# Order of VectorE, GpSimd and opening steps in a two-layer long-convolution and GEGLU kernel

## The chip, the cores and the metric

One core of a Trainium2 chip. The metric is the device time of one execution in microseconds; the runs give 977.12 as the median of three.

## The reference

Two layers run one after the other on `x` (1 x 2048 x 576, bf16). Each layer first gates the normalized `x` with a long convolution, then adds a GEGLU feed-forward. The convolution `y` depends on `A_k`, `A_v` and the filters alone, so both layers use the same `y`.

```python
def _A_ref(q, k, v, shift_k, ssm_k, ssm_D):        # long convolution, gated by q
    k_shift = sum over t of k_pad[:, t:t + S, :] * shift_k[:, ks - 1 - t]   # ks = 4 taps
    kv = k_shift * v
    y = irfft(rfft(kv, 2 * S) * rfft(ssm_k, 2 * S))[:, :S] + kv * ssm_D
    return q * y
def _B_ref(x, w_gate, w_up, w_down):               # 576 -> 4608 -> 576
    return (_gelu(x @ w_gate) * (x @ w_up)) @ w_down
for _ in range(2):
    x = x + _A_ref(_layernorm(x), A_k, A_v, A_shift_k, A_ssm_k, A_ssm_D)
    x = x + _B_ref(_layernorm(x), B_w_gate, B_w_up, B_w_down)
```

## The kernel before

**Units and visits.** The 2048 tokens are four blocks of 512. A unit is a layer and a block, in the order (0,0) (0,1) (1,0) (1,1) (0,2) (0,3) (1,2) (1,3), called unit 0 to unit 7 here. Five passes hold units 0; 1 and 2; 3 and 4; 5 and 6; 7. In each pass the 36 column tiles of the feed-forward are gone through in three parts of twelve; within a part, each unit of the pass is visited once, so there are 24 visits. A visit has twelve gate-and-up tiles ("gu", 18 matmuls each, line 1087), each followed by a GELU on ScalarE (line 1091, tile `ga`) and a product on VectorE (line 1092, tile `hT`), and then four groups of 24 down-projection matmuls ("dn", line 1103), one group for each 128 tokens.

**What a unit needs first.** Before its first visit, each of the four 128-token rows of a unit goes through: two VectorE gate steps with the convolution's `y` (lines 855 and 862, the second also sums the row), the mean's negative `nm` on GpSimd (line 819), a square with a sum on ScalarE (line 827, tile `junk`), `ve` and `rstd` on GpSimd (lines 834 and 835), a normalization `xn` and a short copy on VectorE (lines 888 and 890), and two DMA transposes from SP's queue into `xnT` (line 918). All four rows must have landed before the unit's first gu matmul. Layer 1 has the same steps, with a temporary `g_t`.

**The convolution.** It is a block FFT made of matmuls. For block m: the taps and the product with `v` on VectorE (lines 160 to 170, tiles `kvt` and `v`), forward transforms on TensorE (line 205), whose results ScalarE copies (line 208, `eo`) and VectorE combines (line 213, `kc`); products of spectra on VectorE (lines 222 to 226, `prod` and `sum`, spectra `kr` and `hr` loaded by GpSimd's DMAs, lines 316 and 324); accumulation on TensorE (line 232); and inverse transforms (line 258) copied to `y` (line 260). TensorE's share of this is put between matmuls of the feed-forward. Block 0 is done in the opening, block 1 during unit 0, blocks 2 and 3 later.

**The order.** A planner in Python, run while the program is built, writes the order out. It keeps a modelled time for TensorE, VectorE and ScalarE (`Pace`), with a constant cost for each step (`C_TINY` for a small GpSimd step). VectorE work waits in two lists: `conv.V` with the convolution's steps and `vq` with gates and normalizations. After each gu tile and each pair of dn matmuls `fill` takes from both, as long as modelled VectorE time allows; its argument `conv_first` says which list is asked first. Small GpSimd steps, spills of spectra and output stores wait in `conv.spills` with a due time and are put out by `flush` when modelled TensorE time has reached it. The weight loads (`load_wgu`, 12 tiles' worth in three buffers, lines 745 to 747; `load_wd`, line 755) stand in SP's queue along with the transposes.

```python
hurry = lambda: (1, RT - 1) not in conv.y_at            # block 1's y is not there yet
fill(t.pe + C_GU + LEAD, hurry(), hurry())              # after each gu tile
fill(t.pe + 1.5, True, hurry())                         # after each pair of dn matmuls
```

**The opening** (`Conv.begin`, lines 472 to 673) is ordered by hand: block 0's convolution, spectra of the filter for all four blocks (`h_tile`, matmuls of line 184, copied by ScalarE at line 186, stored to DRAM by GpSimd's queue at line 263; four buffers, so that a later `h_tile` waits for an earlier store), and unit 0's gates and normalizations. There `gate0(j)` does the two gate steps, the mean, the square and the root of row j; `norm0(j)` the normalization (lines 997 and 999); `turn0(j)` transposes it on TensorE (line 1009), with copies of the result (lines 1010 and 1012) on ScalarE or VectorE. One ScalarE table load for GELU is set off by the activation at line 653.

Of the kernel before, what the change touches and what calls it, by code (L numbers as in the profile page):

```python
# [18 lines left out]
P = 128  # L19
# [10 lines left out]
C_GU, C_DN = 1.944, 0.245  # L30
C_PR = 1.25
C_BF, C_TB = 0.37, 0.46
C_SQ, C_TINY = 0.85, 1.0
N_KC, N_SM = 4, 6
C_TT, C_ST, C_BN, C_NORM, C_HT, C_GELU, C_EVA, C_EVD = 0.76, 0.82, 0.47, 0.62, 0.69, 0.6, 0.66, 0.76
LAG = 0.25
HOLD, LEAD = 14.0, 1.8


# [15 lines left out]
class Conv:  # L55
# [9 lines left out]
    def __init__(self, tc, ctx, pace, A_k, A_v, A_shift_k, A_ssm_k, A_ssm_D, ident, psp, cpsp, ypool):  # L65
        self.tc, self.nc, self.t = tc, tc.nc, pace
        self.k2, self.v2, self.hk = A_k[0], A_v[0], A_ssm_k
        self.S, self.D = self.k2.shape
        self.NB = self.S // BS
        self.KS = A_shift_k.shape[1]  # L70
        self.sk, self.sD = A_shift_k, A_ssm_D
        self.ident, self.psp, self.cpsp, self.ypool = ident, psp, cpsp, ypool
        D = self.D
        pool = lambda name, bufs: ctx.enter_context(tc.tile_pool(name=name, bufs=bufs))
        self.cst = pool("c_cst", 1)
        self.krp = pool("c_kr", 3)
        self.hrp = pool("c_hr", 4)
        self.kcp = pool("c_kc", N_KC)
        self.ybp = pool("c_yb", 4 * RT)
        self.prp = pool("c_pr", 3)  # L80
        self.smp = pool("c_sm", N_SM)
        self.eop = pool("c_eo", 2)
        self.kvp = pool("c_kv", 1)
        self.Hd = [[tc.dram_tile([P, 2 * D], BF16, name=f"Hd{b}_{t}") for t in range(RT)] for b in range(self.NB)]
        self.Kd = [[tc.dram_tile([P, 2 * D], BF16, name=f"Kd{b}_{t}") for t in range(RT)] for b in range(self.NB - 1)]
        self.F1 = self.cst.tile([P, RT, 2, 2, P], BF16, name="F1")
        self.F2 = self.cst.tile([P, 2, 2, 2, P], BF16, name="F2")
        self.skc = self.cst.tile([P, self.KS, D], BF16, name="skc")
        self.y, self.yb = {}, {}
        self.kt_, self.vt_ = {}, {}  # L90
        self.y_at = {(0, j): 0.0 for j in range(RT)}
        self.kv_at, self.fwd_at = {}, {}
        self.y_used = {}
        self.startup = True
        self.nps = 0
        self.ps_free = 0.0
        self.pr_free = [0.0] * N_SM
        self.neo = 0
        self.U = deque()
        self.kr_free, self.hr_free = [0.0] * 3, [0.0] * 4  # L100
        self.npr = self.nkr = self.nhr = 0
        self.V, self.L, self.Pq = deque(), deque(), deque()
        self.spills = deque()

    def halves(self, ap):
# [337 lines left out]
    def run_v(self, limit):  # L443

        t = self.t
        if self.U and self.U[0][0] <= t.pe + 0.2 and max(t.dve, t.pe - 1.0) + self.U[0][1] <= limit:
            self.U.popleft()[2]()
            return True
        if not self.V:
            return False  # L450
        ready, cost, run = self.V[0]
        r = ready()
        if r > t.pe + 0.2 or max(t.dve, t.pe - 1.0) + cost > limit:
            return False
        self.V.popleft()
        fin = run()
        fin(t.on_dve(cost, r))
        return True
# [10 lines left out]
        t.pe += cost  # L469
        return True  # L470

    def begin(self, gate0, norm0, turn0, x0_stats, more, scratch, wide, stay):

        tc, nc, D = self.tc, self.nc, self.D
        with ExitStack() as es:
# [143 lines left out]
            def pair0(kt, sg):  # L619
                for part in range(2):  # L620
                    b = self.ybp.tile([P, D], BF16, tag="yb", name="yb")
                    nc.vector.tensor_tensor(out=b[:], in0=A[(part, kt)][:], in1=A[(part, kt + 2)][:],
                                            op=ALU.subtract if sg else ALU.add)
                    self.yb[(part, kt, sg)] = b
# [15 lines left out]
            self.load_v(1, nc.gpsimd)  # L640
            kacc(3)
            pair0(1, 0)
            h_tile(1, 1, self.hrp)
            h_tile(1, 3, self.hrp)
            hT[3] = load_h(3)
# [4 lines left out]
            pair0(1, 1)  # L650
            inv0(1)
            inv0(3)
            nc.scalar.activation(out=warm[:], in_=self.pis[:, 1:2], func=ACT.Gelu_apprx_tanh)
            more(2)
            self.kv1 = self.kv_ops(1)
            ops = iter(self.kv1)
# [1 line left out]
            def kv1_ops(n):  # L658
                for _ in range(n):
                    next(ops)[1]()  # L660
            gate0(0)
            gate0(2)
            h_tile(2, 2, self.hrp)
            h_tile(2, 1, self.hrp)
            gate0(1)
            norm0(0)
            h_tile(2, 3, self.hrp)
            turn0(0, True)
            gate0(3)
            norm0(2)  # L670
            h_tile(3, 0, self.hrp)
            turn0(2, True)
            norm0(1)
            kv1_ops(2)
            h_tile(3, 2, self.hrp)
            norm0(3)
            turn0(1, False)
            kv1_ops(2)
            h_tile(3, 1, self.hrp)
            turn0(3, False)  # L680
            kv1_ops(4)
            h_tile(3, 3, self.hrp)
            more(3)
            self.flush(0.0)
# [4 lines left out]
def ssm_geglu_kernel(ctx, tc, A_q, A_k, A_v, A_shift_k, A_ssm_k, A_ssm_D, B_x, B_w_gate, B_w_up,  # L689
                     B_w_down, out):  # L690
    nc = tc.nc
# [124 lines left out]
    def mean_after(v, when):  # L816
        def run():
            v["nm"] = small.tile([P, 1], F32, tag=v["pfx"] + "nm", name="nm")
            nc.gpsimd.tensor_scalar(out=v["nm"][:], in0=v["s"][:], scalar1=-1.0 / D, scalar2=None, op0=ALU.mult)  # L819
            v["nm_at"] = max(t.pe, when) + C_TINY  # L820
        conv.spills.append((when, run))

    def square_task(get_x, v):
        def run():
            v["ss"] = small.tile([P, 1], F32, tag="ss", name="ss")
            junk = work.tile([P, D], BF16, tag="ga", name="junk")
            nc.scalar.activation(out=junk[:], in_=get_x(), func=ACT.Square, bias=v["nm"][:, 0:1],  # L827
                                 accum_out=v["ss"][:])
            when = t.on_act(C_SQ, t.pe - 1.0) + LAG

            def root():
                ve = small.tile([P, 1], F32, tag="ve", name="ve")
                v["rstd"] = small.tile([P, 1], F32, tag=v["pfx"] + "rstd", name="rstd")
                nc.gpsimd.tensor_scalar(out=ve[:], in0=v["ss"][:], scalar1=1.0 / D, scalar2=EPS, op0=ALU.mult, op1=ALU.add)  # L834
                nc.gpsimd.tensor_tensor(out=v["rstd"][:], in0=ve[:], in1=neghalf_t[:, 0:1], op=ALU.pow)  # L835
                v["rstd_at"] = max(t.pe, when) + 2 * C_TINY
            conv.spills.append((when, root))
        aq.append((at_v(v, "nm_at"), C_SQ, run))

    def run_aq(limit):  # L840
# [148 lines left out]
    with tc.manual_schedule():  # L989
# [9 lines left out]
            nc.vector.tensor_copy(out=xn[:, D:XW], in_=xn[:, 0:HK])  # L999
            xn0[j] = xn  # L1000

        def turn0(j, act):
            if 0 not in xnT_of:
                xnT_of[0] = xtp.tile([P, NKC, CH], BF16, tag="xnT", name="xnT")
            pt = psp.tile([P, 2, 1024], BF16, tag="pr", name="xps")
            tok = slice(j * P, (j + 1) * P)
            for b in range(NKC):
                c0 = b * P if b < 5 else HK + (b - 5) * P
                nc.tensor.transpose(pt[:, b // 5, (b % 5) * P:(b % 5 + 1) * P], xn0[j][:, c0:c0 + P], ident[:])
            (nc.scalar.copy if act else nc.vector.tensor_copy)(  # L1010
                out=xnT_of[0][:, 5:NKC, tok], in_=pt[:, 1, 0:4 * P].rearrange("p (b q) -> p b q", q=P))
            nc.scalar.copy(out=xnT_of[0][:, 0:5, tok], in_=pt[:, 0, 0:5 * P].rearrange("p (b q) -> p b q", q=P))

        xn0 = {}
# [1 line left out]
        def gate0(j):  # L1016
            for _, _, run in gate_steps(0, j, gvars[0][j], vs0[j]):
                run()
            conv.spills.pop()[1]()
            aq.pop()[2]()  # L1020
            conv.spills.pop()[1]()

        def more(k):
            if k == 0:
# [5 lines left out]
                load_wgu(2)  # L1030
            else:
                load_x(1)
        conv.begin(gate0, norm0, turn0, lambda k: [run() for _, _, run in g0[4 * k:4 * k + 4]], more,
                   lambda dt: xtp.tile([P, RT if dt == I32 else 2, D], dt, tag="xnT", name="ang"),
                   lambda: wpool.tile([P, NKC, fw], BF16, tag="wgu", name="hn"),
                   lambda: xpool.tile([P, RT, 2, D], BF16, tag="x", name="H1"))
# [3 lines left out]
        for n in range(3):  # L1040
            load_wd(n)
        conv.step(1, kv=conv.kv1[8:], loaded=True)
        for m in range(2, NCH):
            conv.step(m)

# [8 lines left out]
        for wb, ph, ui, first, final in visits:  # L1054
# [25 lines left out]
            for fi in range(FP):  # L1080
# [12 lines left out]
                free.append(t.on_dve(C_HT, t.on_act(C_GELU, t.pe + 0.15) + 0.15) + 0.1)  # L1093
                if gi == FG - 1 and final:
                    when_due(t.pe + (FP - FG) * C_GU + 12.0, load_wgu, n + 3)
                fill(t.pe + C_GU + LEAD, hurry(), hurry())
            for j in range(RT):
                acc = psp.tile([P, 2, 512], F32, tag="pr", name="dn")
                xa = x_c[c][:, j, :]
# [15 lines left out]
                for fi in range(FP):  # L1115
                    for h in range(2):
                        down(fi, h)
                    t.pe += C_DN
                    if fi < FP - 1:
                        fill(t.pe + 1.5, True, hurry())  # L1120
                if layer == 1 and end:
                    ob = work.tile([P, D], BF16, tag="ob", name="ob")
                    nc.vector.tensor_tensor(out=ob[:].rearrange("p (h d) -> p h d", h=2), in0=xh,  # L1123
# [68 lines left out]
```

## Time and profile before

| | us |
|---|---|
| runs, median (lowest to highest) | 977.12 (976.35 to 979.27) |
| the profiled execution | 973.51 |
| its span, first to last instruction | 971.7 |
| TensorE busy in the span | 949.8 |
| VectorE busy | 537.3 |
| ScalarE busy | 305.4 |
| GpSimd busy | 139.5 |
| first gu matmul starts | 65.82 |

The span is what the trace covers; the profiled execution's own time has 1.81 us around it. Busy times are per engine; engines run beside each other, so the sum is not the span. "PEclk" is the granted TensorE clock as a part of full speed.

### The profile page before, as it was taken

Reading aid. Unit: us, or ns where it says so; the run is one execution under the profiler, and the core shown is the slowest. Engines: PE = TensorE matmul, PEld = TensorE weight load, DVE = VectorE, ACT = ScalarE, POOL = GpSimd, SP = SyncE. Lnnn points to the kernel's source line nnn. Section 1 sums busy time; section 2 is a strip of 40 time slices with the busy share of each in tenths; the row PEclk is TensorE's granted clock in tenths of the full one; section 3 lists DMA queues with packets and bytes.
Section 4 is the critical chain, followed back from the end, with each engine's and each line's share of the span. In section 5 each row is a group of like instructions: output and inputs, shape, how many; then the busy total and the mean of one; then the engine's idle time right before and its main releaser. Section 6 shows DMA issues by size and latency. Waiting matters only on the chain.

```text
span 971.7 us, 19304 instructions
## 1 busy us (share of the span) xinstructions
PE 949.8 (98%) x8256; PEld 547.9 (56%) x8256; DVE 537.3 (55%) x973; ACT 305.4 (31%) x559; POOL 139.5 (14%) x303
## 2 busy tenths in 40 slices
PE   8989999879999999999999999999999999999998
PEld 5755554536556465565565565565565466466455
DVE  8957887858498555879543333564323324533332
ACT  7765213522221533414113322233212213411211
POOL 2353100512020301413000000231000001200000
PEclk9999999989999999999999999999999999999999
DMA  7989975955680740497360270385360450398730
GB/s 180 307 227 291 271 171 134 181 150 123 128 281 22 152 121 14 110 209 189 81 155 16 45 148 30 74 145 125 68 152 1 88 133 1 54 239 170 158 77 26
DMA packets 129067, 127.48 MB, mean 131 GB/s; under 512 B 45588, under 2 KB 121685, under 8 KB 128981
## 3 DMA queue, kind: packets, MB, share of 16 engines
q1 hardware_dynamic: 119904, 90.85, 44.4%
q0 software_dynamic: 8944, 34.49, 11.0%
q8 instruction: 64, 1.05, 0.5%
q10 hardware_dynamic: 132, 0.91, 0.3%
q14 instruction: 23, 0.18, 0.1%
HBM read 105.58 MB, written 10.62 MB: 120 GB/s over the span
## 4 chain that ended last, share of the span: by engine, by line
PE 92%; DVE 4%; DMA 3%; ACT 1%; issue 0%; POOL 0%; ACTq 0%; SPq 0%; DVEq 0%
PE gu L1087 58%; PE dn L1103 28%; PE cps L232 2%; PE cps L258 1%; PE cps L205 1%; DMA k<-in_A_k_dram 1%; DMA xnT<-xn 1%; DMA Hd<-h 1%; DVE kvt L160 1%; PE ps L184 0%; DVE prod L225 0%; DVE yb L226 0%; DVE kvt L165 0%; PE ps L258 0%; DVE stats L771 0%
## 5 line engine op out<-in xcount | busy, mean ns | idle before, releaser
L1087 PE MATMUL gu<-xnT,wgu 64*128 64x512 bf16 x5184 | 568.2, 377 | 7.9 <-DMA xnT<-xn 7.9
L1087 PEld LDWEIGHTS <-wgu 64*128 64x128 bf16 x5184 | 251.4, 94 | 314.8 <-issue 19.3
L1092 DVE TENSOR_TENSOR hT<-ga,gu 128x512 bf16<-128x512 f32 x288 | 197.7, 687 | 282.4 <-ACT ga L1091 281.1
L1091 ACT ACTIVATE ga<-gu 128x512 f32<-128x512 f32 x288 | 171.9, 597 | 545.0 <-PE gu L1087 541.9
L1103 PE MATMUL dn<-wd,hT 128*128 128x288 bf16 x2304 | 297.4, 286 | 0.5 <-DVE ob L1112 0.5
L1103 PEld LDWEIGHTS <-hT 128*128 128x128 bf16 x2304 | 223.3, 98 | 66.4 <-issue 10.5
L1137 DVE TENSOR_TENSOR x_c<-x_c,dn 128x576 f32<-128x576 f32 x64 | 48.2, 753 | 83.2 <-PE dn L1103 82.8
L819 POOL TENSOR_SCALAR nm<-s 128x1 f32<-128x1 f32 x60 | 20.6, 343 | 370.4 <-DVE x_c L1132 160.2
L827 ACT ACTIVATE junk<-x_c,nm 128x576 bf16<-128x576 f32 x48 | 36.9, 769 | 22.2 <-POOL nm L819 22.1
L835 POOL TENSOR_TENSOR rstd<-ve,neghalf_t 128x1 f32<-128x1 f32 x60 | 36.9, 614 | 5.0
L226 DVE TENSOR_TENSOR sum<-prod 128x576 bf16<-128x576 bf16 x72 | 33.0, 458 | 2.7
L184 PEld LDWEIGHTS <-G 128*128 128x128 bf16 x256 | 25.9, 102 | 14.6 <-issue 5.7
L184 PE MATMUL ps<-h,G 128*128 128x288 bf16 x192 | 27.8, 299 | 4.2 <-ACT h L186 3.0
L324 POOL DMA_DIRECT2D hr<-Hd x32 | 17.4, 543 | 73.5 <-DVE prod L225 73.4
L1123 DVE TENSOR_TENSOR ob<-x_c,dn 128x576 bf16<-128x576 f32 x15 | 11.3, 754 | 29.4 <-PE dn L1103 18.4
L834 POOL TENSOR_SCALAR ve<-ss 128x1 f32<-128x1 f32 x60 | 17.7, 296 | 64.8 <-ACT junk L827 64.6
L316 POOL DMA_DIRECT2D kr<-Kd x24 | 13.7, 572 | 85.2 <-DVE prod L225 85.2
L232 PE MATMUL cps<-sum,ident 128*128 128x288 bf16 x144 | 25.3, 287 | 0.0
L160 DVE TENSOR_TENSOR kvt<-k,skc 128x1152 bf16<-128x1152 bf16 x32 | 23.9, 754 | 1.8 <-DMA k<-in_A_k_dram 1.2
L213 DVE TENSOR_TENSOR kc<-eo 128x288 bf16<-128x288 f32 x48 | 19.4, 452 | 2.7 <-ACT eo L208 2.6
L208 ACT COPY eo<-cps 128x576 f32<-128x576 f32 x24 | 15.3, 636 | 16.1 <-PE cps L205 11.9
L266 POOL DMA_DIRECT2D out_dram<-ob x12 | 6.7, 561 | 88.9 <-DVE ob L1123 88.9
(115 smaller groups left out, 471.3 us busy)
## 6 DMA issues: line engine op xcount, KB each, us to landing
wgu<-in_B_w_gate_dram SPq DMA_DIRECT2D x45, 576.0 KB, 5.8
wd<-in_B_w_down_dram SPq DMA_DIRECT2D x30, 864.0 KB, 7.3
wgu<-in_B_w_up_dram SPq DMA_DIRECT2D x45, 512.0 KB, 7.7
hr<-Hd POOLq DMA_DIRECT2D x32, 288.0 KB, 5.5
kr<-Kd POOLq DMA_DIRECT2D x24, 288.0 KB, 4.6
Hd<-h POOLq DMA_DIRECT2D x12, 288.0 KB, 4.2
Kd<-kc POOLq DMA_DIRECT2D x12, 288.0 KB, 8.1
k<-in_A_k_dram POOLq DMA_DIRECT2D x3, 1008.0 KB, 12.2
```

What stands on the lines that cost most here:

```text
L160: nc.vector.tensor_tensor(out=st[dst][:], in0=self.kt_[b][:, s0:s0 + 2, :], in1=self.skc[:, j, :].unsqueeze(1).to_broadcast([P, 2, D]), op ...
L184: nc.tensor.matmul(ps[:, h, 0:HW], lhsT=G[:, i, s * NFQ + kt * P: s * NFQ + (kt + 1) * P], rhs=src[:, i, h * HW:(h + 1) * HW], start=(i == ...
L226: nc.vector.tensor_tensor(out=dst, in0=pr[:, 0, :], in1=pr[:, 1, :], op=ALU.subtract if part == 0 else ALU.add)
L232: nc.tensor.matmul(ps[:, h, 0:HW], lhsT=self.ident[:], rhs=pr[:, h * HW:(h + 1) * HW], start=first, stop=last)
L819: nc.gpsimd.tensor_scalar(out=v["nm"][:], in0=v["s"][:], scalar1=-1.0 / D, scalar2=None, op0=ALU.mult)
L827: nc.scalar.activation(out=junk[:], in_=get_x(), func=ACT.Square, bias=v["nm"][:, 0:1], accum_out=v["ss"][:])
L835: nc.gpsimd.tensor_tensor(out=v["rstd"][:], in0=ve[:], in1=neghalf_t[:, 0:1], op=ALU.pow)
L1087: nc.tensor.matmul(pair[:, s, :], lhsT=w[r0:r0 + HK, k, gi * P:(gi + 1) * P], rhs=xnT[r0:r0 + HK, b, :], start=(k == 0), stop=(k == NKC - 1))
L1091: nc.scalar.activation(out=ga[:], in_=pair[:, 0, :], func=ACT.Gelu_apprx_tanh)
L1092: nc.vector.tensor_tensor(out=hT[:, fi, :], in0=ga[:], in1=pair[:, 1, :], op=ALU.mult)
L1103: nc.tensor.matmul(acc[:, h, 0:HW], lhsT=hT[:, fi, j * P:(j + 1) * P], rhs=wd[2 * wb + fi // WT][:, fi % WT, h * HW:(h + 1) * HW], start=( ...
L1137: nc.vector.tensor_tensor(out=xh, in0=xh, in1=acc[:, :, 0:HW], op=ALU.add)
```

## The change

- `fill` asks the convolution's list first only until block 1's last product of spectra has been taken (`conv.left`, the count of block 1's VectorE steps, set after `step(1)` and lowered as they are taken), and not until block 1's `y` is complete. From then on gates and normalizations are asked for first, and block 2's and 3's convolution steps after them.
- Small GpSimd steps (`nm`, and `ve` with `rstd`) are put out `AHEAD` = 2.0 modelled us sooner, and their modelled cost falls from 1.0 to 0.6.
- In the opening, the GELU table load stands ahead of the `h_tile` copies of block 1. `gate0` is split: its root is now `root0`. Gates 0, 2 and 1 stand together ahead of the `h_tile` matmuls, and the fourth gate one `h_tile` sooner than before; normalizations and turns are spaced otherwise; in each turn the four-block copy is now always on VectorE and the five-block copy on ScalarE; the eight `kvt` steps that stand there come later.

```diff
-C_SQ, C_TINY = 0.85, 1.0
+C_SQ, C_TINY = 0.85, 0.6
+AHEAD = 2.0
...
         self.V.popleft()
+        self.left -= 1
...
             pair0(1, 0)
+            nc.scalar.activation(out=warm[:], in_=self.pis[:, 1:2], func=ACT.Gelu_apprx_tanh)
             h_tile(1, 1, self.hrp)
...
-            nc.scalar.activation(out=warm[:], in_=self.pis[:, 1:2], func=ACT.Gelu_apprx_tanh)
             more(2)
...
             gate0(0)
             gate0(2)
+            root0(0)
+            root0(2)
+            gate0(1)
+            root0(1)
             h_tile(2, 2, self.hrp)
+            norm0(0)
             h_tile(2, 1, self.hrp)
-            gate0(1)
-            norm0(0)
+            gate0(3)
+            root0(3)
+            norm0(2)
+            turn0(0)
             h_tile(2, 3, self.hrp)
-            turn0(0, True)
-            gate0(3)
-            norm0(2)
+            turn0(2)
+            norm0(1)
             h_tile(3, 0, self.hrp)
-            turn0(2, True)
-            norm0(1)
+            turn0(1)
+            norm0(3)
             kv1_ops(2)
             h_tile(3, 2, self.hrp)
-            norm0(3)
-            turn0(1, False)
-            kv1_ops(2)
+            turn0(3)
+            kv1_ops(6)
             h_tile(3, 1, self.hrp)
-            turn0(3, False)
-            kv1_ops(4)
             h_tile(3, 3, self.hrp)
...
-        conv.spills.append((when, run))
+        conv.spills.append((when - AHEAD, run))
...
-            conv.spills.append((when, root))
+            conv.spills.append((when - AHEAD, root))
...
-            (nc.scalar.copy if act else nc.vector.tensor_copy)(
-                out=xnT_of[0][:, 5:NKC, tok], in_=pt[:, 1, 0:4 * P].rearrange("p (b q) -> p b q", q=P))
+            nc.vector.tensor_copy(out=xnT_of[0][:, 5:NKC, tok], in_=pt[:, 1, 0:4 * P].rearrange("p (b q) -> p b q", q=P))
...
-            conv.spills.pop()[1]()
+            roots[j] = conv.spills.pop()[1]
+
+        roots = {}
+        root0 = lambda j: roots[j]()
...
         conv.step(1, kv=conv.kv1[8:], loaded=True)
+        conv.left = len(conv.V)
...
-                fill(t.pe + C_GU + LEAD, hurry(), hurry())
+                fill(t.pe + C_GU + LEAD, hurry(), conv.left > 0)
...
-                        fill(t.pe + 1.5, True, hurry())
+                        fill(t.pe + 1.5, True, conv.left > 0)
```

More of the change, by code (lines that the diff above doesn't have):

```diff
@@ L102, in __init__ @@
         self.V, self.L, self.Pq = deque(), deque(), deque()
+        self.left = 0
         self.spills = deque()
@@ L470, in run_p, with begin @@
         return True
-    def begin(self, gate0, norm0, turn0, x0_stats, more, scratch, wide, stay):
+    def begin(self, gate0, root0, norm0, turn0, x0_stats, more, scratch, wide, stay):
         tc, nc, D = self.tc, self.nc, self.D
@@ L1000, in norm0, with turn0 @@
             xn0[j] = xn
-        def turn0(j, act):
+        def turn0(j):
             if 0 not in xnT_of:
@@ L1032, in more @@
                 load_x(1)
-        conv.begin(gate0, norm0, turn0, lambda k: [run() for _, _, run in g0[4 * k:4 * k + 4]], more,
+        conv.begin(gate0, root0, norm0, turn0, lambda k: [run() for _, _, run in g0[4 * k:4 * k + 4]], more,
                    lambda dt: xtp.tile([P, RT if dt == I32 else 2, D], dt, tag="xnT", name="ang"),
```

## The prediction

> **What bounds the kernel now.** I read the page's totals first, then TensorE's waits, then busy time by stage, then the chain and the timeline where the waits are.
>
> ```profile
> span 971.7 us, 19304 instructions
> PE 949.8 (98%) x8256; PEld 547.9 (56%) x8256; DVE 537.3 (55%) x973; ACT 305.4 (31%) x559; POOL 139.5 (14%) x303
> ```
>
> TensorE is busy for 949.8 of 971.7 us. The change adds and removes no matmul, so it can only touch the other 21.9 us, or make new idle time. TensorE's waits (what it waited for: us in total, times, longest) say where the old idle time is:
>
> ```profile
> PE gu L1087 <- DMA xnT<-xn: 7.9, 1, 7.9
> ```
>
> One wait of 7.9 us in front of a unit stands above all others; the rest lie in the opening. By stage (stage, its length, then TensorE's busy time, further on PEclk, the granted clock):
>
> ```profile
> 42.14:65.82 23.68, 19.59 (x176) 15.22 (x173) 15.44 (x32) 18.15 (x33) 10.74 (x20) 1.00 0.85 228
> 65.82:174.75 108.93, 108.93 (x938) 56.87 (x937) 85.31 (x152) 38.20 (x72) 19.89 (x40) 1.00 0.86 221
> 174.75:199.49 24.74, 16.42 (x133) 12.63 (x131) 16.32 (x42) 9.56 (x19) 10.95 (x24) 0.94 0.92 197
> 199.49:340.00 140.51, 140.51 (x1229) 77.40 (x1230) 100.81 (x181) 42.20 (x81) 25.70 (x52) 0.99 0.55 138
> 340.00:560.00 220.00, 220.00 (x1935) 127.88 (x1935) 125.18 (x232) 65.84 (x124) 29.47 (x66) 1.00 0.47 104
> ...
> 199.40:200.50 1.10, 1.01 (x6) 0.37 (x8) 0.00 (x0) 0.00 (x0) 0.00 (x0) 0.50 1.10 335
> ...
> 204.00:206.00 2.00, 2.00 (x22) 0.90 (x20) 1.78 (x4) 0.66 (x3) 0.21 (x1) 1.00 0.13 37
> ```
>
> From 65.82 to 174.75 and from 199.49 to 560 TensorE is never idle: whatever the change reorders there can lose time and cannot gain any. Two stages have something to give, 42.14 to 65.82 (the end of the opening) and 174.75 to 199.49 (the hand-over from unit 0 to unit 1). In the second the chain reads (start, length, what):
>
> ```profile
> 189.58 9.22 DMA xnT<-xn
> ...
> 199.49 25.33 PE gu L1087 x216
> ...
> 238.65 23.41 PE gu L1087 x216
> ...
> 567.60 11.87 PE dn L1103 x96
> ```
>
> TensorE is ready at 199.49 - 7.91 = 191.58 and waits for the last transposes of unit 1. Then its clock is granted at 0.50 and is full again by 204, and the visit's 216 matmuls take 25.33 instead of 23.41: the stall is worth 7.91 + 1.92 = 9.83 us.
>
> **Part 1, gates of unit 1 first.** Why the transposes are late (start, length, engine, line):
>
> ```profile
> 156.37 0.69 DVE L1092 TENSOR_TENSOR hT<-ga,gu 128x512 bf16<-128x512 f32 x1 [1.66 <-ACT ga L1091]
> ...
> 163.09 0.65 ACT L260 ACTIVATE y<-cps 128x576 bf16<-128x576 f32 x1 [0.48 <-PE cps L258]
> ...
> 166.38 0.81 DVE L855 SCALAR_TENSOR_TENSOR x_c<-x_b,nm,y 128x576 f32<-128x576 bf16 x1
> ...
> 167.29 0.82 DVE L862 SCALAR_TENSOR_TENSOR x_c<-x_c,rstd,x_b 128x576 f32<-128x576 f32 x1
> ...
> 174.75 0.42 PE L1103 MATMUL dn<-wd,hT 128*128 128x288 bf16 x2
> ...
> 179.49 0.75 DVE L1132 SCALAR_TENSOR_TENSOR x_c<-dn,x_c 128x576 f32<-128x576 f32 x1
> ...
> 180.78 0.62 SPq L745 DMA_DIRECT2D wgu<-in_B_w_gate_dram  x1
> ...
> 183.19 11.48 SPq L918 DMA_TRANSPOSE xnT<-xn  x6
> ...
> 189.36 0.57 DVE L888 TENSOR_SCALAR xn<-x_c,nm,rstd 128x576 bf16<-128x576 f32 x1
> ```
>
> Block 1's last `y` is there at 163.74, but the first gate step begins at 166.38 and the last `xn` at 189.36: the convolution's list was asked first. In the order of instructions of the changed program the gate pairs of rows 0, 1 and 2 stand directly behind the fourth, fifth and sixth `hT` of unit 0's last visit; `xn` of row 0 and the first step of row 3 behind the eighth; row 3's second step and row 1's `xn` behind the ninth; row 2's `xn` behind the tenth; row 3's `xn` behind the first L1132 of the dn groups. The fourth `hT` stands at 156.37 here, so the pairs (0.81 + 0.82 = 1.63) run from 157.1, 160.2 and 163.3. Row 3's second step then ends near 172. Only four block-2 `kvt` steps and the product with `v` still come between (five times some 0.75, by the row below), all ahead of L1132. The first dn group ends near 177.7 (174.75 + 24 matmuls of 11.87 / 96 = 0.124), VectorE is through with `kvt` and `v` near 178.4, L1132 ends near 179.2, and the last `xn` with its copy near 180. That is 9.5 us sooner than 189.36 + 0.75.
>
> ```profile
> L160 DVE TENSOR_TENSOR kvt<-k,skc 128x1152 bf16<-128x1152 bf16 x32 | 23.9, 754 | 1.8 <-DMA k<-in_A_k_dram 1.2
> ...
> wgu<-in_B_w_up_dram SPq DMA_DIRECT2D x45, 512.0 KB, 7.7
> hr<-Hd POOLq DMA_DIRECT2D x32, 288.0 KB, 5.5
> kr<-Kd POOLq DMA_DIRECT2D x24, 288.0 KB, 4.6
> ```
>
> With the old 9.22 us from the end of VectorE's work to the landing, `xnT` is complete by 189.2, still 2.4 us before TensorE is ready; and the old 9.22 had two weight loads ahead of it in the rings, which now follow behind. So I take the whole 9.8 us. What hides what is pushed back: SP's queue now has two of the three `wgu` groups behind all eight transposes, which take 11.48 / 6 = 1.9 us each there; after the last pair the groups issue from about 183.8, where the later of them issued at 180.78 before. The first is wanted at the fifth gu tile, 191.6 + 4 x 23.41 / 12 = 199.4; three issues of 0.62 and 7.7 to land make 193.4: 6 us of cover. The second is wanted 7.8 us later. Block 2's forward transforms begin some 4 us later inside the dn groups; the stretch takes 191.58 - 174.75 = 16.83 us now, against 11.87 of dn matmuls and 30 of the convolution's in between (0.124 each, 3.7): 1.3 us of small waits on `eo` and `kc`. I keep them at 1.3; the bounds are none and twice that. Next late in this stage is then the plain matmul sequence itself.
>
> **Part 2, the opening.**
>
> ```profile
> 40.55 0.65 ACT L186 ACTIVATE h<-ps 128x576 bf16<-128x576 f32 x1 [0.33 <-PE ps L184]
> ...
> 42.34 0.65 ACT L260 ACTIVATE y<-cps 128x576 bf16<-128x576 f32 x1 [1.14 <-PE cps L258]
> ...
> 45.95 1.28 ACT L653 ACT_TABLE_LOAD   x1
> ...
> 47.35 0.76 ACT L827 ACTIVATE junk<-x_c,nm 128x576 bf16<-128x576 f32 x1
> 47.40 0.82 DVE L791 SCALAR_TENSOR_TENSOR x_c<-x_c,rstd,x_b 128x576 f32<-128x576 f32 x1
> ...
> 50.13 0.63 ACT L186 ACTIVATE h<-cps 128x576 bf16<-128x576 f32 x1
> ...
> 50.81 1.14 PE L184 MATMUL cps<-h,G 128*128 128x288 bf16 x8 [1.65 <-ACT h L186]
> ...
> 51.92 1.32 POOL L263 DMA_DIRECT2D Hd<-h  x2
> ...
> 58.86 1.19 ACT L186 ACTIVATE h<-ps 128x576 bf16<-128x576 f32 x2 [1.03 <-DMA Hd<-h]
> ...
> 65.82 4.49 PE L1087 MATMUL gu<-xnT,wgu 64*128 64x512 bf16 x40
> ```
>
> The table load leaves 45.95 to 47.35 on ScalarE, 1.40 us, and goes in front of six copies that each have 0.33 us of slack (1.98 in all) and another 1.14 before the first `y`: moved, it costs nothing. The Trainium skill, "ScalarE: Activation LUTs", What ACT_TABLE_LOAD costs, charges about 2.66 us a switch, a load of 1.28 and a drain of 1.38; this trace has 1.40 from the load's start to the next square, so here no drain shows. By the page the freed time would be 2.7 instead of 1.4, and at the new place 2.7 stands against 1.98 + 1.14: still hidden.
>
> The freed 1.40 is used up at once: three squares instead of two now stand ahead of the `h` copies, and the third waits for a gate step that ended at 48.22 and for GpSimd, so the copies resume near 50.05, as before (50.13). What follows gains. From 50.81 to 65.82 TensorE had two more waits on `h` copies, 2.4 us in all (its waits in the window 42 to 66):
>
> ```profile
> PE ps L184 <- ACT h L186: 2.4, 2, 1.3
> ```
>
> The later one hangs on a GpSimd store: issued at 51.92, landed at 58.8 and waited for by ScalarE at 58.86. In the new order that store follows the third row's root, near 51.0, and lands 0.9 sooner. Bounds: all 2.4 of waits gone, or none. Nearest to the store's row I take 1.5, a first gu at 64.3. It could lose if the store lands later; 1 us at worst, since the loads beside it are unmoved.
>
> **Part 3, GpSimd steps sooner.** From 199.49 to 560 no TensorE wait ends on them, so the gain is nil. The cost when the cover goes: a step that stands up to 2 us early on GpSimd holds up what is queued behind it, the `kr` and `hr` loads and the spills. These land in 4.6 and 5.5 us where the planner's step counts on 8.0 (`at[("ld", kt, a)] = t.pe + 8.0`), so 2.5 us of cover stand against 2.0. I take zero; without the cover, each late load would cost the wait priced under the second rival.
>
> **The sum.** 973.51 - 9.8 - 1.5 = 962.2 for a profiled execution (span about 960.4). The median of the runs is 3.6 above the profiled one (977.12 - 973.51), and I carry that over: 965.8 us.
>
> **Rivals.** *A part of the stall stays.* If VectorE runs behind, for instance because the fourth to sixth `hT` slip, `xn` moves out and with it transposes and the two `wgu` groups queued behind. For it: the queue order is now stricter. Against: 2.4 us of margin by the old landing time. With 3 to 6 us left, 969 to 972. The Trainium skill, "TensorE: Matmul & The Clock Gate", The HAM clock gate, has half clock only after an idle window of about 3.4 us; the trace agrees in that the 1.65 us wait of the opening left PEclk at 1.00, the 7.91 one took it to 0.50. *Reordering is paid for later.* Block 2's and 3's products now yield to every gate and normalization, and VectorE is 72% busy from 199.49 to 340 (100.81 of 140.51). TensorE takes the accumulations in order, so a late product stops the dn matmuls too. It ends slower than before by over 0.3% from 11.3 + 2.9 = 14.2 us of new waits on: in the new order eight visits after unit 0's still carry convolution, so 1.8 us in each, a little over the 1.65 us wait of the opening. Then about 980 us. Against it:
>
> ```profile
> L1092 DVE TENSOR_TENSOR hT<-ga,gu 128x512 bf16<-128x512 f32 x288 | 197.7, 687 | 282.4 <-ACT ga L1091 281.1
> ```
>
> VectorE sits idle 281.1 us ahead of 288 `hT` until ScalarE is done: it catches up nearly once a tile. *The change does not reach the stall.* If unit 1's last row were still behind the dn groups nothing but the opening is gained, 975.6; the instruction order speaks against it.
>
> **How the numbers follow.** Forecast 0.73; part of the stall stays 0.14; paid later 0.07; not reached 0.06. This kernel's measurement tells about 0.3%, 2.9 us, from no change. Faster by more takes the first two: 0.87; within it 0.06; slower 0.07. The forecast's own range is 962.0 (opening 2.4, small dn waits 1.3 gone, and half of the 2.9 between the lowest and the highest run) to 968.6 (opening nothing, dn waits 1.3 more). With the part-stall case the range is 962.0 to 971.0.
>
> **What would show it.** Right: no wait of gu on `xnT` anywhere, PEclk at 1.00 around 190, the last `xn` of unit 1 near 180, the second visit's 216 gu matmuls in 23.4, first gu near 64.3. Wrong: gu waiting on `wgu` near 199, dn waiting on `eo` or `sum` after 191, or a first gu later than 65.8.

## The result, and the profile after

| | before | after |
|---|---|---|
| runs of one chip, median (lowest to highest) | 977.0 (976.35 to 979.27, 4 runs) | 964.67 (962.89 to 965.51, 4 runs) |
| ratio after to before, 95% interval | | 0.9867 (0.9846 to 0.9889) |
| the profiled execution | 973.51 | 965.51 |
| first gu matmul of unit 0 | 65.82 | 68.15 |
| first gu matmul of unit 1 | 199.49 | 192.68 |

The changed kernel is faster by 1.3%, 12.3 us between the medians against 11.3 forecast. The profile's totals for it:

```profile
span 963.7 us, 19315 instructions
PE 948.0 (98%) x8256; PEld 546.6 (57%) x8256; DVE 538.8 (56%) x975; ACT 304.5 (32%) x557; POOL 139.7 (14%) x303
```

TensorE is nearly as busy as before (948.0 us against 949.8); its idle time went from 21.9 to 15.7 us. Its longest waits in the changed kernel (waited for: us in total, times, longest), down to 1.2 us:

```profile
PE hps L551 <- DMA hn<-in_A_ssm_k_dram: 3.6, 1, 3.6
PE xps L1015 <- ACT h L188: 3.2, 1, 3.2
PE ps L186 <- DVE h L553: 1.2, 1, 1.2
```

The 7.9 us wait of gu on `xnT` is gone. Two waits are new or longer, and both lie in the opening: one of 3.2 us on a ScalarE copy, and one of 3.6 us on the first filter load, which was 0.8 in the profile of before. By stage (stage, length, TensorE's busy time, further on the granted clock):

```profile
42.14:64.30 22.16, 18.48 (x157) 14.47 (x155) 15.10 (x35) 14.75 (x27) 9.33 (x18) 0.92 0.93 254
...
172.00:200.00 28.00, 27.98 (x240) 17.50 (x238) 24.44 (x55) 13.38 (x27) 11.88 (x25) 1.00 0.85 157
200.00:340.00 140.00, 140.00 (x1234) 80.77 (x1231) 101.14 (x184) 43.05 (x79) 23.18 (x48) 1.00 0.62 159
```

The hand-over from unit 0 to unit 1 (172 to 200) has 0.02 us of idle TensorE and full clock, and nothing is lost behind it (140.00 of 140.00). In the opening, though, the granted clock is now 0.92 on average, where it was 1.00 before; this is taken up under "The opening, alone". The steps of the hand-over, from the timeline and, in the last two rows, from the chain (which starts these two pieces 0.06 to 0.07 us after the timeline's first matmul; times of first matmuls in the text are the timeline's):

```profile
158.70 0.69 DVE L1101 TENSOR_TENSOR hT<-ga,gu 128x512 bf16<-128x512 f32 x1 [1.65 <-ACT ga L1100]
...
159.31 0.81 DVE L861 SCALAR_TENSOR_TENSOR x_c<-x_b,nm,y 128x576 f32<-128x576 bf16 x1
...
180.91 0.58 DVE L894 TENSOR_SCALAR xn<-x_c,nm,rstd 128x576 bf16<-128x576 f32 x1
...
184.35 0.61 SPq L751 DMA_DIRECT2D wgu<-in_B_w_gate_dram  x1
```

```profile
68.22 15.65 PE gu L1096 x144
...
192.74 23.42 PE gu L1096 x216
```

Unit 1's first gate step comes right behind the fourth `hT`, the last `xn` at 180.91, the weight loads right behind the transposes, and the second visit's 216 matmuls take 23.42 us. The eight transposes of unit 1 landed 2.6 us after their issue (median) where they had taken 7.7 before.

Where the 8.0 us between the two spans came from: up to the first gu the changed kernel's execution is 2.33 us later (65.82 to 68.15); from there to unit 1's first gu it takes 124.53 instead of 133.67 us, 9.14 less; that visit takes 23.42 instead of 25.33, 1.91 less; what is left, 0.7, comes back as work: the dn groups ahead of unit 1 hold 28 of block 2's matmuls instead of 34, and the six stand later.

### The profile page after: what moved, and what is told of

It is laid out like the page before. It is cut to its first block, busy times and chain, and to the rows that moved or that the text cites. A ratio compares the mean times of both kernels' runs of the same rounds, so it can differ in the third digit from the quotient of the medians.

```text
span 963.7 us, 19315 instructions
## 1 busy us (share of the span) xinstructions
PE 948.0 (98%) x8256; PEld 546.6 (57%) x8256; DVE 538.8 (56%) x975; ACT 304.5 (32%) x557; POOL 139.7 (14%) x303
## 4 chain that ended last, share of the span: by engine, by line
PE 95%; DVE 3%; DMA 1%; ACT 1%; POOL 0%; issue 0%; SPq 0%; DVEq 0%
PE gu L1096 58%; PE dn L1112 30%; PE cps L234 2%; PE cps L207 1%; PE cps L260 1%; PE ps L186 1%; DMA hn<-in_A_ssm_k_dram 1%; PE cps L186 0%; DVE yb L228 0%; DVE prod L227 0%; DVE yb L625 0%; DVE stats L777 0%; DVE kvt L162 0%; DVE prod L224 0%; PE xps L1015 0%
## 5 line engine op out<-in xcount | busy, mean ns | idle before, releaser
L1132 DVE TENSOR_TENSOR ob<-x_c,dn 128x576 bf16<-128x576 f32 x15 | 11.3, 755 | 29.0 <-PE dn L1112 19.9
```

## The experiments

Each is compared with the kernel before on the same chip, and each profile is one execution. Since the wait for the first filter load turned out to change from execution to execution (below), the opening is measured from unit 0's first gate step on VectorE to the first gu matmul, behind that load. This stretch is 22.59 us in the kernel before (43.23 to 65.82) and 22.53 in the changed one (45.62 to 68.15; the expectations below have 22.60, counted to the chain's 68.22).

**Gates first, alone.** The kernel before with the one edit of the list order.

```diff
         self.V.popleft()
+        self.left -= 1
...
         conv.step(1, kv=conv.kv1[8:], loaded=True)
+        conv.left = len(conv.V)
...
-                fill(t.pe + C_GU + LEAD, hurry(), hurry())
+                fill(t.pe + C_GU + LEAD, hurry(), conv.left > 0)
...
-                        fill(t.pe + 1.5, True, hurry())
+                        fill(t.pe + 1.5, True, conv.left > 0)
```

> Only the order of gates against block 2's convolution steps is changed; the opening and the small GpSimd steps are as before. Theory (the gates' place removes the stall at the hand-over to unit 1): the 7.9 us wait of gu on xnT and the half-clock stretch behind it are gone, 9.8 us less than the kernel before, 966 to 968 us, with the first gu where it was. Rival (the three parts are needed together): 3 to 5 us of the wait stay, 970 to 973 us.

Measured: 964.56 us, 1.4 us under the expected range, ratio 0.9885 (0.9868 to 0.9902). No wait of gu on `xnT`; in the chain, the visit with 23.41:

```profile
193.17 23.41 PE gu L1090 x216
```

So this one edit gives the whole gain that the measurement can see: its interval and that of the full change (0.9846 to 0.9889) overlap.

**GpSimd steps sooner, alone.**

```diff
-C_SQ, C_TINY = 0.85, 1.0
+C_SQ, C_TINY = 0.85, 0.6
+AHEAD = 2.0
...
-        conv.spills.append((when, run))
+        conv.spills.append((when - AHEAD, run))
...
-            conv.spills.append((when, root))
+            conv.spills.append((when - AHEAD, root))
```

> Only the small GpSimd steps are changed (put out 2.0 us sooner, modelled cost 0.6); gates and opening as before. Theory (no TensorE wait ends on them): within 0.3% of the kernel before, and the wait of gu on xnT stays between 6 and 9 us. Rival (they hold the normalizations of unit 1 back): the last normalization comes 2 us or more sooner and the wait falls below 6 us, 972 us or less.

Measured: 966.58 us, ratio 0.9911 (0.9891 to 0.993). This went against the prediction's third part. TensorE's wait, and the timeline:

```profile
PE gu L1088 <- DMA xnT<-xn: 2.1, 1, 2.1
```

```profile
185.39 0.58 DVE L889 TENSOR_SCALAR xn<-x_c,nm,rstd 128x576 bf16<-128x576 f32 x1
...
195.09 2.09 PE L1088 MATMUL gu<-xnT,wgu 64*128 64x512 bf16 x16 [2.08 <-DMA xnT<-xn]
```

The last `xn` stands at 185.39 instead of 189.36, in an execution whose first gu is 1.90 us later (67.72), so 5.9 us sooner; the wait falls by 5.8, from 7.9 to 2.1 us. In the window right behind the wait the clock (the third figure from the right) is still full:

```profile
195.00:197.00 2.00, 1.90 (x16) 0.82 (x18) 0.00 (x0) 0.00 (x0) 0.00 (x0) 1.00 0.89 228
```

The planner takes a normalization only when its root has been put out and is done by the modelled time (`v["rstd_at"] = max(t.pe, when) + 2 * C_TINY`). Put out sooner, the roots are known sooner, and in the order of instructions the last `xn` moves from behind the third of the L1132 steps of the dn groups to behind the second. The next two runs part the two edits.

**Put out sooner only** (`AHEAD` = 2.0, `C_TINY` still 1.0), and **cost only** (`C_TINY` 0.6, no `AHEAD`).

```diff
+AHEAD = 2.0
...
-        conv.spills.append((when, run))
+        conv.spills.append((when - AHEAD, run))
...
-            conv.spills.append((when, root))
+            conv.spills.append((when - AHEAD, root))
```

```diff
-C_SQ, C_TINY = 0.85, 1.0
+C_SQ, C_TINY = 0.85, 0.6
```

> The kernel before with one thing of the change: means and roots are put out on GpSimd 2.0 modelled us sooner; their modelled cost stays 1.0. In the order of instructions the last row's xn of unit 1 then stands where it stood with both small edits together, behind the second L1132 step of the dn groups instead of the fourth. Theory (being put out sooner is what lets the planner take the normalizations sooner): like both small edits together, so a wait of gu on xnT of at most 3 us, the clock at 1.00 behind it, a median of 966 to 968 us, ratio 0.990 to 0.992. Rival (only both edits together do it, the cost taken for a root decides): the wait stays at 5 to 8 us, 973 us or more, ratio above 0.996.

> The kernel before with the other thing: the modelled cost of a small GpSimd step falls from 1.0 to 0.6, and they are put out no sooner. The last xn of unit 1 moves ahead of the third L1132 step only, one dn group sooner in the order. Theory: the last xn stays late by 5 us or more against being put out sooner, the wait of gu on xnT stays at 4 to 8 us, clock at 0.50 behind it, 971 to 976 us, ratio 0.995 to 1.000. Rival (the cost alone moves the normalizations enough): a wait of 3 us or less, ratio below 0.993.

Measured: 969.26 us, ratio 0.9923 (0.9906 to 0.994) for the first, 974.65 us, 0.9989 (0.9976 to 1.0001) for the second. TensorE's wait at the hand-over, first and second:

```profile
PE gu L1088 <- DMA xnT<-xn: 2.2, 1, 2.2
```

```profile
PE gu L1087 <- DMA xnT<-xn: 8.2, 1, 8.2
```

(The last `xn` stood behind the third L1132 step in the kernel before, not the fourth, as the first expectation has it.) Putting the steps out sooner is what helps; the cost that the planner counts does nothing to the wait. It does move the last `xn`; rows from the second kernel's timeline and chain:

```profile
187.66 0.57 DVE L888 TENSOR_SCALAR xn<-x_c,nm,rstd 128x576 bf16<-128x576 f32 x1
```

```profile
192.18 7.69 DMA xnT<-xn
```

In an execution whose first gu is 1.01 us later, that is an `xn` 2.7 us sooner than 189.36, and 3.2 us behind that of the kernel with the steps sooner (5 or more were expected). But the third row's `xn` stayed where it was (185.45 against 184.44), and the last row's transposes stand behind the third row's in SP's queue: their first was issued at 192.18 here and at 191.36 before, the same within 0.2 us on one scale. So the stall does not hang on the last `xn` alone, but on all late rows and on how fast the queue passes their transposes on. The median of the kernel with the steps sooner is 1.3 us above the 968 that was expected, but its interval overlaps that of both edits together, and the wait is the same.

**The opening, alone.** All edits between the table load and the last turn, nothing else:

```diff
+            nc.scalar.activation(out=warm[:], in_=self.pis[:, 1:2], func=ACT.Gelu_apprx_tanh)
             h_tile(1, 1, self.hrp)
...
             gate0(0)
             gate0(2)
+            root0(0)
+            root0(2)
+            gate0(1)
+            root0(1)
             h_tile(2, 2, self.hrp)
...
```

> Only the opening is changed. By the prediction it is worth 1.5 us, 975.5 us, with the first gu 1.5 us sooner. By the trace of the changed kernel the opening gives nothing: the third square waits for GpSimd, TensorE stands 3.2 us once instead of 1.7, 1.1 and 1.3 us: then 977.0 us, within 0.5 us of the kernel before. The 7.9 us wait at the hand-over stays in both.

Measured: 974.74 us, ratio 0.9987 (0.9974 to 1.0001); the stretch is 22.66 us. The medians lie 1.5 us apart, but the interval includes no change, and the stretch is as long as before: the opening's edits gain nothing that can be told. Its waits, and the changed kernel's timeline, say why:

```profile
PE gu L1092 <- DMA xnT<-xn: 8.0, 1, 8.0
PE xps L1012 <- ACT h L186: 3.2, 1, 3.2
```

```profile
51.29 0.78 POOL L841 TENSOR_TENSOR rstd<-ve,neghalf_t 128x1 f32<-128x1 f32 x1
...
52.05 0.63 POOL L825 TENSOR_SCALAR nm<-s 128x1 f32<-128x1 f32 x1
52.71 0.77 ACT L833 ACTIVATE junk<-x_c,nm 128x576 bf16<-128x576 f32 x1 [1.99 <-POOL nm L825]
...
53.49 0.63 ACT L188 ACTIVATE h<-cps 128x576 bf16<-128x576 f32 x1
...
54.60 1.16 POOL L265 DMA_DIRECT2D Hd<-h  x2
54.71 1.12 PE L1015 MATMUL xps<-ident,xn 128*128 128x128 bf16 x9 [3.16 <-ACT h L188]
55.62 2.12 PE L186 MATMUL cps<-h,G 128*128 128x288 bf16 x8
```

The third row's mean stands on GpSimd behind two roots and is made at 52.05; ScalarE's third square waits 1.99 us for it, and behind this square on ScalarE stand the `h` copies, which resume at 53.49. Less the 2.39 by which this execution is late at its first gate step, that is 51.10, against 50.13 before. TensorE now has one wait of 3.16 us where it had three of 1.65, 1.14 and 1.30, so 0.9 us less idle time in all. But the clock falls to 0.50 behind the long wait: the eight `cps` matmuls take 2.12 us where eight took 1.14 before. The stretch before and in the changed kernel, by stage as above (length, TensorE's busy time, and third from the right the granted clock):

```profile
43.23:65.82 22.59, 18.50 (x167) 14.34 (x164) 14.35 (x29) 17.50 (x32) 10.74 (x20) 1.00 0.84 219
```

```profile
45.62:68.15 22.53, 19.37 (x165) 15.24 (x164) 15.36 (x32) 15.71 (x28) 10.37 (x20) 0.92 0.79 205
```

TensorE is busy 0.9 us longer with the same work, which uses up the 0.9 us of idle time that went. Three variants of the changed kernel test this reading.

**The third mean ahead of the roots.**

```diff
+            gate0(1)
             root0(0)
             root0(2)
-            gate0(1)
             root0(1)
```

> The changed kernel with the roots of rows 0 and 2 put behind row 1's mean on GpSimd in the opening. From the first gate step of unit 0 to its first gu matmul the kernel before takes 22.59 us and the changed kernel 22.60. Theory (in the changed kernel the third square waits for its mean, which stands behind two roots on GpSimd, and the spectra's copies stand behind the square on ScalarE): the square comes 1.5 us sooner, TensorE's wait of 3.2 us falls to about 1.8 and the stretch to 21.2 us. Rival (the stretch hangs on GpSimd's stores or on the amount of matmuls): it stays at 22.4 us or more.

Measured: 962.88 us, ratio 0.9879 (0.9857 to 0.9901); the stretch is 21.87 us (43.10 to 64.97). In between: the third square comes about 1.8 us sooner (5.32 us after the first gate step instead of 7.09) and the wait on the copies shrank, but more than that came back behind it. TensorE is idle for 3.6 us of this stretch, more than the changed kernel's 3.2; what is gained is the clock, which stays at 1.00, with 18.26 us of busy time instead of 19.37.

```profile
PE ps L186 <- ACT xnT L1017: 1.4, 1, 1.4
PE xps L1015 <- ACT h L188: 1.4, 1, 1.4
PE ps L186 <- ACT h L188: 1.4, 2, 0.8
```

**The third gate behind the first `h_tile`.**

```diff
             root0(2)
+            h_tile(2, 2, self.hrp)
             gate0(1)
             root0(1)
-            h_tile(2, 2, self.hrp)
             norm0(0)
```

> The changed kernel with the third gate of the opening back behind the first spectrum, so that two copies stand ahead of the third square on ScalarE. Theory (as for the kernel with the means first): TensorE's wait on the copies falls from 3.2 to under 1 us, and the stretch from unit 0's first gate step to its first gu matmul from 22.6 to between 20 and 21.2 us. Rival (something else ends the stretch): 22.4 us or more.

Measured: 961.6 us, ratio 0.9866 (0.9845 to 0.9888); the stretch is 21.17 us (43.06 to 64.23). The copies of the first `h_tile` no longer stand behind the third square, and the wait of the transposes on them is 0.3 us:

```profile
48.07 0.63 ACT L188 ACTIVATE h<-cps 128x576 bf16<-128x576 f32 x1
...
49.29 0.66 PE L1015 MATMUL xps<-ident,xn 128*128 128x128 bf16 x9 [0.30 <-ACT h L188]
...
51.00 0.77 ACT L833 ACTIVATE junk<-x_c,nm 128x576 bf16<-128x576 f32 x1 [1.77 <-POOL nm L825]
```

The square waits for GpSimd as before (1.77 us), now with the copies ahead of it. Of the 1.36 us that the stretch is shorter than in the changed kernel, 1.12 are busy time at the full clock and 0.24 idle time:

```profile
43.06:64.23 21.17, 18.25 (x165) 14.36 (x163) 15.26 (x32) 15.30 (x28) 10.68 (x20) 1.00 0.88 224
```

**The table load back in its old place**, all else as in the changed kernel.

```diff
-            nc.scalar.activation(out=warm[:], in_=self.pis[:, 1:2], func=ACT.Gelu_apprx_tanh)
             h_tile(1, 1, self.hrp)
...
+            nc.scalar.activation(out=warm[:], in_=self.pis[:, 1:2], func=ACT.Gelu_apprx_tanh)
             more(2)
```

> The changed kernel with the GELU table load back in its old place, ahead of unit 0's squares. Theory (the third square, held by GpSimd, sets when the copies resume, so the 1.4 us that the moved load freed were used up): the stretch from unit 0's first gate step to its first gu matmul stays at 22.6, within 0.4. Rival (the table load's place is worth its 1.4 us, and something else in the opening cost as much): 24.0 us.

Measured: 963.9 us, ratio 0.9882 (0.986 to 0.9903); the stretch is 23.01 us (43.61 to 66.62). The load's 1.40 us on ScalarE are worth 0.4 to 0.5 us of the stretch, by one profile of this kernel against two of the changed one (22.53 above, 22.65 below): the third square waits for GpSimd in any case, here 1.83 us, and the clock falls behind a TensorE wait of 3.63 us as it does there.

**Both once more on one chip**: the changed kernel, and the one with the third gate later.

> The changed kernel once more, beside the one with the third square later. Expected: ratio 0.987 (0.985 to 0.989) against before; from unit 0's first gate step on VectorE to the first gu matmul 22.6 us (22.4 to 22.8), as in the kernel before (22.59).

> The changed kernel with the third gate (its square and root) behind the first h_tile, once more, beside the changed kernel on the same chip. Theory (a third square ahead of the h copies holds these up by GpSimd's queue): the stretch from the first gate step to the first gu is 21.2 us again (21.0 to 21.5), 1.4 us less than in the changed kernel, and the median lies 1 to 2 us below the changed kernel's, ratio 0.985 to 0.986. Rival (the earlier run's shorter stretch was run-to-run variation, or is lost again later): stretch 22 us or more, or no difference between the medians.

Measured: 964.28 us (963.07 to 966.17), ratio 0.9878 (0.9861 to 0.9896), and 962.16 us (961.41 to 965.31), ratio 0.9861 (0.9842 to 0.988). The stretches are 22.65 (42.88 to 65.53) and 21.19 us (43.96 to 65.15): 1.4 us less in both pairs of profiles, with the clock at 0.92 and 1.00 on average again. The medians lie 2.1 us apart, with overlapping ranges. So a better opening exists, by 1.4 us on the profiles; the whole times agree with it, but alone they would not settle it.

**The weights held back.** The kernel before, with the third group of weight loads kept behind unit 1's transposes in SP's queue; VectorE's order is untouched.

```diff
+            if due[0][2] is load_wgu and due[0][3] == 11 and xn_done.get(1, 0) < RT:
+                break
```

> The kernel before, with one weight group (three loads) that stood between unit 1's first and second pair of transposes in SP's queue put behind the fourth pair; VectorE's order is as before. Rival theory (the last transposes took 9.2 us to land because a weight load was ahead of them in the rings): they land 4 to 6 us sooner, the wait falls to 2 to 4 us and the clock stays full, 969 to 972 us. My theory (the last normalization comes too late on VectorE, and eight transposes in a row need their time anyway): the wait stays at 6 us or more, 975 to 977 us.

Measured: 972.5 us, ratio 0.9965 (0.9953 to 0.9977), between the two theories: TensorE's waits on `xnT` are 5.6 and 0.4 us, and the clock falls. The last `xn` is as late as before, the last transposes take less, and TensorE still waits; rows from the timeline, the chain, the timeline and the windows:

```profile
189.14 0.58 DVE L888 TENSOR_SCALAR xn<-x_c,nm,rstd 128x576 bf16<-128x576 f32 x1
```

```profile
191.20 6.68 DMA xnT<-xn
```

```profile
196.96 0.61 PE L1089 MATMUL gu<-xnT,wgu 64*128 64x512 bf16 x2 [5.60 <-DMA xnT<-xn]
```

```profile
199.00:201.00 2.00, 2.00 (x14) 0.74 (x11) 0.00 (x0) 0.00 (x0) 0.00 (x0) 0.50 1.12 202
```

So the weight loads in front of the transposes account for some 2 us of the 7.9. The rest goes away when the normalizations come sooner (5.7 us of it with the GpSimd steps put out sooner and the weight loads left where they were), and not when only the last one does.

**The kernel before, once more.**

> The kernel before once more, for a second profile. The profiled execution of before was 3.5 us below its other runs. Theory (the filter's first load in the opening varies from run to run): TensorE's wait on hn, 0.8 us in the first profile of before and 3.6 us in that of the changed kernel, differs again by some us, and the span moves with it; all else agrees within 0.5 us. Rival (the difference is spread over the run): the wait on hn is the same and the span differs all the same. Ratio of times 1.000 either way.

Measured: 975.58 us, ratio 1.0 (0.9986 to 1.0014). The stall is 8.3 us in this profile; the wait for the filter load is 3.0 us where it was 0.8.

## Why the prediction was right, point by point

**Part 1, the stall (9.8 us): right.** Each step shows: first gate step at 159.31, which is 157.0 without the 2.3 that this execution is late (157.1 forecast); the last `xn` with its copy done at 181.71, or 179.4 (near 180 forecast); the weight loads from 184.35, or 182.0 (183.8 forecast), with no wait of gu on them. The clock's part is shown too: 25.33 fell to 23.42, 1.91 us. The Trainium skill, "TensorE: Matmul & The Clock Gate", The HAM clock gate, has half clock after at least one idle window of about 3.4 us. The runs agree in that a 2.1 us wait left the clock at 1.00 and waits of 5.6 and 7.9 us took it to 0.50, but the 3.16 us waits of the opening took it to 0.50 too; where they differ, the measurement decides. Two readings on the way were off without touching the sum: near 180 is 10.1 us sooner than 189.36 + 0.75, not 9.5, and the transpose of the 9.22 us row was issued at 189.58, before the last `xn`'s copy ended at 190.15, so that row is not the time from the end of VectorE's work. A smaller term was mis-sized: I put 1.3 us of small waits into the dn groups of this visit, and the trace of before has 0.41 us of idle TensorE there (16.42 busy of 16.83); the rest was busy time, with 34 convolution matmuls where I had counted 30. After, the idle time is 0.02.

**Part 2, the opening (1.5 us, bounds 2.4 and minus 1): wrong; it gave nothing.** The two later waits that I priced did go, all 2.4 us of them. The step that failed concerns the wait ahead of them: "the copies resume near 50.05, as before". I saw that the third square would wait for GpSimd, but priced only the gate step ahead of it, not the two roots that now stand in front of its mean. The copies resume 1.0 us later than before on the same scale, and TensorE's first wait grows from 1.65 to 3.16 us. Behind it comes a term that the sum does not have: this wait takes the clock to 0.50, and TensorE is busy 0.9 us longer. Idle time 0.9 less, busy time 0.9 more, nothing gained. "Moved, it costs nothing" held for the table load; that it frees 1.40 us did not, it frees 0.4 to 0.5. Moving the third gate alone recovers 1.4 us, close to the 1.5 forecast, but for another reason: 1.1 to 1.2 of it are the clock.

**Part 3, GpSimd steps (nil): right beside part 1, wrong as a reading of the mechanism.** Alone they bring a ratio of 0.9911, most of the gain of the whole change. The step that failed: I looked for TensorE waits on these steps from 199.49 to 560 and found none, but not at the hand-over, where the planner holds a normalization back until its root is put out. With gates first the stall is gone already, so nothing is left for them to gain.

**The sum: 965.8 against 964.67, in part by errors that cancel.** The opening's 1.5 us did not come. The 3.6 us that I carried over from the profiled execution to the median were no property of the kernel: the profile of before happened to wait 0.8 us for its first filter load where its repetition waited 3.0 and the changed kernel's 3.6, and for the changed kernel the profiled execution (965.51) is the slowest of its runs instead of the fastest. (The lower end of the range, by its own terms, is 962.1 and not 962.0.) Between medians the change brings 12.3 us, against 9.8 for the stall. Gates first alone has 0.9868 to 0.9902, which is 9.6 to 12.9 us of 976: the stall's price lies within. The traces are tighter: from the first gu to the end of the span, the kernel before takes 905.9 and 906.2 us in its two profiles, the opening alone and the cost alone 905.8 and 905.9, and all seven profiles with gates first 895.6 to 897.0, which is 8.8 to 10.6 us less. The rest of the difference between the medians would then lie ahead of the first gu. The opening's stretch gained nothing, so the first loads may have landed sooner in those runs, which is not shown.

**The rivals.** *A part of the stall stays* and *not reached* are refuted by the missing wait, *paid later* by 140.00 of 140.00 and 220.00 of 220.00 busy in the two stages behind, and by 3.9 us of idle time from 560 to the end both before and after:

```profile
340.00:560.00 220.00, 220.00 (x1942) 125.08 (x1941) 123.84 (x227) 64.83 (x123) 30.75 (x68) 1.00 0.44 104
```

## What to carry to other kernels

A stall at a hand-over is best priced from the row where the waiting engine was ready, with its re-warmed clock added, and the order of instructions then says whether the late work really moves ahead. When small steps on a side engine are moved, look at every place where the planner holds work back for them, and at what stands ahead of them in that engine's own queue. Ask not only how much idle time an order leaves but how it is divided: here two roots of GpSimd in front of one mean made one long wait out of three short ones, with less idle time in all, and the half clock behind the long one took the gain back. An offset between one profiled execution and the median should be explained by a wait before it is carried into a forecast.

## What the runs showed of the hardware

The first DMA loads of an execution land at different times from one execution to the next, with the same instructions around them. The same wait was 3.6 us in the changed kernel (shown above); in the kernel before and in the changed kernel's second run it was:

```profile
PE hps L548 <- DMA hn<-in_A_ssm_k_dram: 0.8, 1, 0.8
```

```profile
PE hps L551 <- DMA hn<-in_A_ssm_k_dram: 0.6, 1, 0.6
```

Over all profiles of this case it goes from none to 3.8 us, and it shifts all that follows. That is of the size of the spread between the runs of one kernel, and larger than all that the opening's edits were about, so such edits have to be measured from a point behind the load.

Behind unit 0's first gate step, a TensorE wait of 3.16 us was enough to take its granted clock to 0.50 in all three profiles that have one (the changed kernel twice, the opening alone), as were waits of 3.63, 5.6, 7.9 and 8.2 us; waits of 2.1 and 2.2 us at the hand-over, and of up to 1.65 us in the opening, left it at 1.00. In the changed kernel's second run and in the opening alone, nine transposes behind the wait still took 0.66 and 0.67 us at full clock, and the clock fell some half to one us after TensorE was at work again. The price was 0.9 to 1.2 us of busy time behind 3.16 us (against the kernel before, and against the third gate later), and 1.9 us behind 7.9 us.
